# Scores of two neighbouring quads in one burst of 64 small matmuls, in a kernel with two attentions

## The chip, the cores and the metric

The kernel runs on one core of a Trainium2 chip. Its time is that of one launch on the device, in microseconds (us), and the median of several launches counts. A core has a matrix engine (PE, with the loading of weights shown as PEld), a vector engine (DVE), a scalar engine (ACT), GpSimd (POOL), and the sync engine (SP), which here issues nearly all transfers to sixteen DMA engines. Each works through its own list of instructions in order, and they wait for each other by semaphores.

## The reference

Two attention blocks, A and B, on 16 batches of 32 tokens with 1024 features, 32 query heads of 128 and caches of 1024 keys. In A eight query heads share one of 4 key heads; in B each of the 32 heads has its own. Their outputs stand side by side.

```python
q = (x @ wq).reshape(B, Sq, H, Dh).transpose(0, 2, 1, 3)
scores = einsum("bhqd,bhkd->bhqk", q, k_cache) * Dh ** -0.5
p = softmax(scores, axis=-1)
o = einsum("bhqk,bhkd->bhqd", p, v_cache)
return o.transpose(0, 2, 1, 3).reshape(B, Sq, H * Dh) @ wo
```

B's caches are the bulk of the bytes: 128 MB of keys and as many of values (in MiB), against 16 and 16 for A and 8 for each of the four weights.

## The kernel before, in words

The unit of work is a quad: four pairs of batch and head, 4 x 32 = 128 query rows. Each attention has 128 quads, and step t of the main loop (near line 1090) takes quad t of B (`quadB_all`) and about one of A (`quadA_all`). A quad of B is two neighbouring batches times two heads; `hp` says which two of a group's four heads, so that quads t and t + 1 (t even) share their batches and differ in `hp`.

The stages of a quad are: scores into PSUM (`st_scores`: L836 for A, L856 for B), negated row maximum on DVE (L866), exp on ACT with the row sum (L879), transposes of P on PE (L891), copy of them to SBUF (L540, on ACT or DVE), P.V on PE (`st_pv`: L913 for A, L921 for B), scaling by one over the sum (L937 on ACT, L938 on DVE), transpose of the output (L943) and its copy. After four quads of B or eight of A the output projection (L712) is accumulated in SBUF (L723, L726).

*B's keys.* Two K buffers belong to a quad (512 KB each; eight in all, `NKB_SLOTS`), loaded by L781. DVE transposes each buffer in place in 32 x 32 blocks (L815). The score matmuls are small, 32 rows by 32 columns of weights with 512 columns streamed: query rows from `QR`, one `tile_position` of PE's 4 x 4 grid of 32 x 32 tiles each. A quad is 32 of them, as four program entries of eight: entry `fp` goes over two batches, two heads and two halves of the keys. Row group `2 * hh + g2` and column group `2 * t_ + hh` make eight of the sixteen tiles, the same eight for every quad:

```python
for t_ in range(2):
    for hh in range(2):
        cg = 2 * t_ + hh
        for g2 in range(2):
            rg = 2 * hh + g2
```

*B's values.* Three V buffers of 1 MB (`NVB_SLOTS`), two transfers each, L794. Quad t + 2's V is loaded once quad t - 1's P.V has read its buffer. K of quad t + 4 is loaded once quad t's scores have read theirs.

*PSUM.* Two buffers of two banks hold scores (`ps_s`) and are used in turn by all quads of A and B; four banks (`ps_g`) serve all the rest.

*The order.* Nothing runs in the order written. Every operation is recorded with its reads and writes, and `Prog.list_schedule` sorts them by a table of expected durations (`DUR`), priorities from the longest path of users, and an estimate of the transfers; a copy may go to ACT or DVE (`"any"`). At each choice it takes, of the operations that can start within `LOOK` of the earliest, the one with the highest priority, with a penalty for changing PE's tile shape (`PE_MODE`, `MODE_SWITCH`). The result fixes each engine's list, and `finalize` puts in the waits. SP's list is in order too: a transfer whose buffer isn't free holds up those behind it.

*Q projection.* It is cut into units (`qprojA_head`, L624; `qprojB`, L643), each of eight matmuls of 512 columns; the lists `QB0`, `QA0`, `QB1`, `QA_T`, `QB_T` give the steps at which the units of the next heads are recorded.

Of the kernel before, what the change touches and what calls it, by code (L numbers as in the profile page):

```python
# [18 lines left out]
NKB_SLOTS = 8  # L19
LAZY_PER_STEP = 100  # L20
LAZY_DELAY = 4
WQ_DELAY = 1
A_STEPS_FRAC = 0.97
SP_STRICT = False
# [3 lines left out]
PRIO_BONUS = {}  # L28
PE_MODE = {"scoresB": 2, "Qshuf": 2, "Qshuf2": 2, "PVB": 1}
MODE_SWITCH = 0.05  # L30
LOOK = 0.35
STEP_US = 3
STEP_NEAR = 0
# [1 line left out]
TAIL_GAIN = 1.0  # L35
TAIL_BASE = 12.0
QB0 = [0, 3, 6, 9]
QA0 = [13 + (i * 9) // 8 for i in range(8)]
QB1 = [24 + (i * 9) // 8 for i in range(8)]
QA_T = [3 + (i * 12) // 8 for i in range(8)]  # L40
QB_T = [18 + (i * 12) // 8 for i in range(8)]
ACT_FIRST = 0.3


DUR = {
    "scoresB": (0.216, 0.20), "scoresA": (0.216, 0.20), "PT_trA": (0.49, 0.22), "PT_trB": (0.49, 0.22), "PVA": (0.45, 0.22), "PVB": (0.112, 0.22),
    "OT_tr": (0.056, 0.22), "KTA_tr": (0.45, 0.22), "Qshuf": (0.15, 0.20), "Qshuf2": (0.15, 0.20), "qprojA": (0.432, 0.20), "qprojB": (0.432, 0.20),
    "oprojA": (0.432, 0.20), "oprojB": (0.432, 0.20), "xT_tr": (0.45, 0.22),
    "exp": (1.10, 0.12), "PT_ev@act": (0.466, 0.13), "norm@act": (0.25, 0.13), "OT_ev@act": (0.11, 0.13), "KTA_ev@act": (0.466, 0.13),
# [66 lines left out]
class Prog:  # L116
# [118 lines left out]
    def list_schedule(self, lat=0.05, look=LOOK):  # L235
# [87 lines left out]
        def sw(i):  # L323
            if ops[i].eng != "pe":
                return 0.0
            return MODE_SWITCH if PE_MODE.get(ops[i].name, 0) != pe_mode[0] else 0.0

        def occ(i, eng):
            return dict(ops[i].alts)[eng] if ops[i].alts else ops[i].dur
        while True:  # L330
            best = None
            bkey = None
            for eng, lst in ready.items():
                if not lst:
                    continue
                fe = free.get(eng, 0.0)
                if eng == "sp":
                    fe = max(fe, dma_free[0] - SP_AHEAD)
                if eng == "dve":
                    fa = free.get("act", 0.0)  # L340
                    lst = [i for i in lst if not ops[i].alts or max(ready_t[i], fa) > max(ready_t[i], fe) + ACT_FIRST]
                    if not lst:
                        continue
                at = {}
                for i in lst:
                    s_ = slot_time(i) if acq[i] else 0.0
                    if s_ is not None:
                        at[i] = max(ready_t[i], fe, s_) + sw(i)
                if not at:
                    continue  # L350
                emin = min(at.values())
                cand = [i for i in at if at[i] <= emin + look]
                ci = max(cand, key=lambda i: (bl[i] - 8.0 * sw(i), -i))
                st = at[ci]
                end = st + occ(ci, eng)[0] if ops[ci].alts else st
                key = (st, end, -bl[ci])
                if bkey is None or key < bkey:
                    bkey = key
                    best = (ci, eng)
            if best is None:  # L360
                break
            best, beng = best
            op = ops[best]
            for x in engines(op):
                ready[x].remove(best)
            chosen[best] = beng
            st = max(ready_t[best], free.get(beng, 0.0), slot_time(best) if acq[best] else 0.0) + sw(best)
            acquire(best, st)
            if beng == "sp":
                st = max(st, dma_free[0] - SP_AHEAD)  # L370
            if beng == "pe":
                pe_mode[0] = PE_MODE.get(op.name, 0)
            op.t0 = st
            if op.dma_key is not None:
                free[beng] = st + DMA_ISSUE
                xs = max(st + DMA_FIRST, dma_free[0])
                dma_free[0] = xs + dma_time(op)
                op.t1 = dma_free[0] + DMA_LAST
            else:
                oc, tl = occ(best, beng)  # L380
                free[beng] = st + oc
                op.t1 = st + oc + tl
            release(best, op.t1 + lat)
            order.append(best)
            for u in users[best]:
                uo = ops[u]
                same_pe = (op.dma_key is None and beng == uo.eng and uo.eng == "pe" and uo.name != "Qshuf2")
                r = free[beng] if same_pe else op.t1 + lat
                if uo.dma_key is not None:
                    r += DMA_MARGIN.get(uo.name, DMA_MARGIN_DEFAULT)  # L390
                if r > ready_t[u]:
                    ready_t[u] = r
                ndeps[u] -= 1
                if ndeps[u] == 0:
                    make_ready(u)
# [54 lines left out]
def build(nc, pa, pb, out):  # L450
# [34 lines left out]
    with stack:  # L485
# [212 lines left out]
        def oproj(pi, blk, G):  # L698
# [3 lines left out]
            OT = OTA_sb if pi == 0 else OTB_sb  # L702
            wo_ = woA_sb if pi == 0 else woB_sb
            wo_res = "woA" if pi == 0 else "woB"
            lazy_flush(("wo", pi, blk))
            for oh in range(NOH):
                v = Virt("bank", "pj")
                for h0_ in range(0, nh, 2):
                    def e_op(e, oh=oh, h0_=h0_, v=v):
                        last = None  # L710
                        for hh in range(h0_, h0_ + 2):
                            last = e.matmul(bank(v)[:, 0:OUTW], OT[:, gp, hh, :], wo_[:, hh, oh * OUTW:(oh + 1) * OUTW],  # L712
                                            start=(hh == 0), stop=(hh == nh - 1))
                        return last
                    pr.add("pe", e_op, reads=[("OT", pi, gp, h0_), ("OT", pi, gp, h0_ + 1), (wo_res, h0_), (wo_res, h0_ + 1)], writes=[v],
# [106 lines left out]
                self.idx = idx  # L822
                self.res = [("bank", 2 * idx), ("bank", 2 * idx + 1)]

        def st_scores(q):
            q.vS = SBuf(s_rr[0] % 2)
            s_rr[0] += 1
            q.vP, q.vPT, q.vst, q.vO = Virt("P"), Virt("PT"), Virt("stat"), Virt("O")
            q.vbt, q.vbo = Virt("bank"), Virt("bank")
            vS = q.vS  # L830
            if q.pi == 0:
                sl = q.kvslot
                qt = QT_sb[:, q.s % 2]

                for u in range(2):
# [1 line left out]
                                                         KTA_sb[:, sl, u * 512:(u + 1) * 512], start=True, stop=True),  # L837
                           reads=[("QT", q.s % 2, q.hh0 + a) for a in range(4)] + [("KTA", sl)], writes=vS.res, name="scoresA", dur=0.225,
                           tag="A%d" % q.t, rtag=dict([(("QT", q.s % 2, q.hh0 + a), q.s) for a in range(4)] + [(("KTA", sl), q.kid)]))
            else:  # L840
                gp = (q.m * NG + q.G) % 2

                def e_s(e, fp):
                    last = None
                    if True:
                        f, pd = fp // 2, fp % 2
                        o0 = f * 64 + pd
                        for t_ in range(2):
                            a = 2 * q.bp + t_
                            for hh in range(2):  # L850
                                cg = 2 * t_ + hh
                                for g2 in range(2):
                                    rg = 2 * hh + g2
                                    lhsT = QR[32 * rg:32 * rg + 32, gp, a, q.hp, o0:o0 + 63:2]
                                    rhs = KB_sb[32 * rg:32 * rg + 32, q.ks[t_], :].rearrange("p (s x) -> p s x", s=16)[:, :, o0:o0 + 63:2]
                                    last = e.matmul(ps_s[32 * cg:32 * cg + 32, vS.idx, g2, :].rearrange("p (s j) -> p s j", s=16), lhsT, rhs,  # L856
                                                    start=(fp == 0), stop=(fp == 3), tile_position=(32 * rg, 32 * cg))
                    return last
                for fp_ in range(4):
                    pr.add("pe", lambda e, fp_=fp_: e_s(e, fp_), reads=[("QR", gp, 2 * q.bp), ("QR", gp, 2 * q.bp + 1), ("KB", q.ks[0]), ("KB", q.ks[1])],  # L860
                           writes=vS.res, name="scoresB", dur=0.275, tag="B%d" % q.t,
                           rtag={("QR", gp, 2 * q.bp): (q.m, q.G), ("QR", gp, 2 * q.bp + 1): (q.m, q.G), ("KB", q.ks[0]): ("T", q.kid), ("KB", q.ks[1]): ("T", q.kid)})

        def st_max(q):
            vS, vst = q.vS, q.vst
# [37 lines left out]
        def st_pv(q):  # L903
# [12 lines left out]
            else:  # L916
                def e_pv(e, c0):
                    last = None
                    for c in range(c0, c0 + 2):
                        for a in range(4):  # L920
                            last = e.matmul(bank(vb)[32 * a:32 * a + 32, 0:Dh], ptc_of(vPT, c, 32 * a, 32 * a + 32), VB_sb[:, kvs, a // 2, a % 2, c, :],  # L921
                                            start=(c == 0), stop=(c == NCH - 1), tile_position=(0, 32 * a))
                    return last
                for c0 in range(0, NCH, 2):
# [43 lines left out]

        def quadB_all(q):
            t = q.t  # L970
            for t_ in range(2):
                st_ktrB(q, t_)
            if t >= 1 and t - 1 + NVB < NIT:
                st_dmaV(quadsB[t - 1 + NVB])
            if t in (0, 1) and t + 2 < NIT:
                for t_ in range(2):
                    st_dmaK(quadsB[t + 2], t_)
            st_scores(q)
            if t + NKB // 2 < NIT:
                for t_ in range(2):  # L980
                    st_dmaK(quadsB[t + NKB // 2], t_)
            st_max(q)
            st_exp(q)
            st_ptr(q)
# [6 lines left out]
        def quadA_all(q):  # L991
            t = q.t
            if q.kv_new:
# [5 lines left out]
                        st_dmaK(n3)  # L999
                if n1 is not None and t >= 1:  # L1000
                    st_dmaV(n1)
            st_scores(q)
            st_max(q)
            st_exp(q)
            st_ptr(q)
# [150 lines left out]
```

## Time and profile before

| | |
|---|---|
| three runs, median | 889.17 us (888.12 to 889.93) |
| the profiled execution, its own time | 889.07 us |
| its span, first to last instruction | 887.3 us |
| granted TensorE clock, mean | 0.996 |
| HBM read, written | 337.64 MB, 2.10 MB |
| issue to landing, median, of a K or V transfer of B | 12.5, 12.2 us |
| shortest | 7.3, 7.0 us |

The profile page gives the busy time of each engine, the span in 40 slices (a digit is the busy share in tenths, and below them the GB/s that the DMA engines moved), the DMA queues, the chain of work that ended last, and groups of instructions by line: busy time, mean duration of one in ns, and the idle time just before them with what ended it. Busy time of matmuls is merged where they overlap. An answer by stretches has in each row the stretch, its length, busy time and count for PE, PEld, DVE, ACT and POOL, the granted clock, the DMA share and GB/s. A timeline row has start, length, engine, line, operation, tile and how many instructions are merged in it.

### The profile page before, as it was taken

The page shows a single profiled execution, that of the slowest core. Times are in us where ns is not written, and L with a number is a line of the kernel's source. Part 1 is how long each engine was busy: PE and PEld are TensorE (multiplying, and loading weights), DVE is VectorE, ACT ScalarE, POOL GpSimd, SP SyncE. Part 2 cuts the span into 40 slices and gives each one's busy share as a digit, 9 for nine tenths or more (in the row PEclk, how much of TensorE's full clock was granted, in tenths as well). Part 3 has the DMA queues.
Part 4 walks back from the last instruction along what each step waited for, and adds up shares of the span by engine and source line. Part 5 has one row for each costly group of instructions (what it writes and reads, how often), then busy time and mean ns, then how long its engine had stood idle before and what let it go on. Part 6 is the DMA issues. An engine that isn't in the chain of part 4 may idle for free.

```text
span 887.3 us, 29315 instructions
## 1 busy us (share of the span) xinstructions
PE 817.8 (92%) x12864; PEld 468.8 (53%) x12864; DVE 737.1 (83%) x1027; ACT 609.4 (69%) x1350; POOL 5.1 (1%) x15
## 2 busy tenths in 40 slices
PE   6999999999999999999999999999999887988986
PEld 3355555556555555555555455554555544554643
DVE  0498987879987888888898888898989888898985
ACT  3487886776767576775776677676767766676763
POOL 0000000000000000000000000000000000000000
PEclk9999999999999999999999999999999999999999
DMA  8999999999999999999999999999999999999995
GB/s 316 397 395 391 394 393 396 390 392 395 394 381 387 396 394 387 385 392 395 395 392 394 389 394 396 369 395 393 395 396 364 392 395 395 395 395 389 397 395 207
DMA packets 144830, 341.65 MB, mean 385 GB/s; under 512 B 12032, under 2 KB 12032, under 8 KB 144704
## 3 DMA queue, kind: packets, MB, share of 16 engines
q1 hardware_dynamic: 144144, 337.95, 100.6%
q8 instruction: 101, 1.65, 0.8%
q0 software_dynamic: 560, 1.84, 0.5%
q14 instruction: 25, 0.20, 0.1%
HBM read 337.64 MB, written 2.10 MB: 383 GB/s over the span
## 4 chain that ended last, share of the span: by engine, by line
PE 56%; DMA 19%; DVE 10%; ACT 8%; SPq 4%; issue 1%; ACTq 0%; DVEq 0%
DMA KB_sb<-in_B_k_cache_dram 16%; PE ps_s L856 12%; PE ps_g L891 9%; PE ps_g L712 8%; ACT P_sb L879 5%; PE ps_g L921 5%; PE ps_g L624 5%; DVE stat L866 5%; DVE KB_sb L815 4%; PE ps_g L643 4%; PE ps_g L913 4%; PE ps_s L836 4%; PE ps_g L807 2%; SPq L794 2%; PE ps_g L943 1%; ACT PT_sb L540 1%
## 5 line engine op out<-in xcount | busy, mean ns | idle before, releaser
L866 DVE TENSOR_REDUCE stat<-ps_s 128x1 f32<-128x1024 f32 x256 | 305.6, 1208 | 53.9 <-PE ps_s L856 44.5
L815 DVE STREAM_TRANSPOSE KB_sb<-KB_sb 128x1024 f32<-128x1024 f32 x256 | 309.4, 1229 | 36.6 <-DMA KB_sb<-in_B_k_cache_dram 34.4
L879 ACT ACTIVATE P_sb<-ps_s,stat 128x1024 bf16<-128x1024 f32 x256 | 286.4, 1120 | 58.8 <-DVE stat L866 57.1
L891 PE MATMUL ps_g<-id,P_sb 128*128 128x128 f32 x1024 | 172.9, 296 | 10.8 <-ACT OTA_sb L540 3.8
L856 PE MATMUL ps_s<-KB_sb,QR 32*32 32x512 bf16 x4096 | 159.1, 396 | 20.9 <-ACT P_sb L879 15.3
L891 PEld LDWEIGHTS ps_g<-id,P_sb 128*128 128x128 f32 x1024 | 148.8, 207 | 49.4 <-issue 8.3
L540 ACT COPY PT_sb<-ps_g 128x512 f32<-128x512 f32 x238 | 138.2, 593 | 46.9 <-PE ps_g L891 45.8
L937 ACT ACTIVATE O_sb<-ps_g,stat 128x128 bf16<-128x128 f32 x189 | 68.9, 371 | 64.0 <-PE ps_g L921 36.8
L921 PE MATMUL ps_g<-VB_sb,PT_sb 128*32 128x128 bf16 x4096 | 90.7, 222 | 4.6 <-ACT PT_sb L540 2.2
L836 PE MATMUL ps_s<-KTA_sb,QT_sb 128*128 128x512 bf16 x256 | 87.1, 383 | 4.6 <-ACT P_sb L879 4.4
L856 PEld LDWEIGHTS ps_s<-KB_sb,QR 32*32 32x32 bf16 x4096 | 47.4, 89 | 82.5 <-ACT P_sb L879 24.1
L921 PEld LDWEIGHTS ps_g<-VB_sb,PT_sb 128*32 128x32 bf16 x4096 | 59.8, 97 | 52.9 <-issue 36.8
L913 PE MATMUL ps_g<-VA_sb,PT_sb 128*128 128x128 bf16 x1024 | 77.6, 220 | 3.6 <-DMA VA_sb<-in_A_v_cache_dram 1.3
L913 PEld LDWEIGHTS ps_g<-VA_sb,PT_sb 128*128 128x128 bf16 x1024 | 60.9, 98 | 32.0 <-issue 13.4
L643 PE MATMUL ps_g<-wq_sb,xT_sb 128*128 128x512 bf16 x256 | 73.2, 390 | 3.5 <-DMA wq_sb<-in_B_wq_dram 3.5
L712 PE MATMUL ps_g<-woB_sb,OTB_sb 128*128 128x512 bf16 x256 | 68.1, 380 | 2.7 <-ACT PT_sb L540 1.3
L712 PE MATMUL ps_g<-woA_sb,OTA_sb 128*128 128x512 bf16 x256 | 63.0, 380 | 1.2 <-DVE OTA_sb L540 0.6
L943 PE MATMUL ps_g<-ident,O_sb 128*128 128x128 bf16 x256 | 52.3, 223 | 4.9 <-ACT O_sb L937 4.2
L624 PE MATMUL ps_g<-xT_sb,wq_sb 128*128 128x512 bf16 x192 | 55.5, 380 | 0.8 <-DMA wq_sb<-in_A_wq_dram 0.5
L879 ACT ACTIVATION_READ_ACCUMULATOR P_sb<-ps_s,stat 128x1 f32 x256 | 51.9, 203 | 0.0
L723 DVE TENSOR_TENSOR acc<-acc,ps_g 128x512 f32<-128x512 f32 x64 | 41.0, 676 | 9.9 <-PE ps_g L712 9.6
L540 ACT COPY OTA_sb<-ps_g 128x64 f32<-128x64 f32 x114 | 24.6, 217 | 35.5 <-PE ps_g L943 34.9
(43 smaller groups left out, 515.0 us busy)
## 6 DMA issues: line engine op xcount, KB each, us to landing
VB_sb<-in_B_v_cache_dram SPq DMA_DIRECT2D x256, 512.0 KB, 12.2
KB_sb<-in_B_k_cache_dram SPq DMA_DIRECT2D x256, 512.0 KB, 12.5
KA_sb<-in_A_k_cache_dram SPq DMA_DIRECT2D x64, 256.0 KB, 12.3
VA_sb<-in_A_v_cache_dram SPq DMA_DIRECT2D x64, 256.0 KB, 12.3
wq_sb<-in_B_wq_dram SPq DMA_DIRECT2D x16, 512.0 KB, 10.5
woB_sb<-in_B_wo_dram SPq DMA_DIRECT2D x32, 256.0 KB, 11.2
woA_sb<-in_A_wo_dram SPq DMA_DIRECT2D x32, 256.0 KB, 10.6
wq_sb<-in_A_wq_dram SPq DMA_DIRECT2D x12, 512.0 KB, 11.4
```

Source lines behind the costliest of these rows:

```text
L540: return e.copy(dst, src) if hasattr(e, "activation") else e.tensor_copy(dst, src)
L624: last = e.matmul(bank(v)[:, 0:tn], w_[:, j, hh * Dh:(hh + 1) * Dh], xT_sb[:, 0, j, t0:t0 + tn], start=(j == 0), stop=(j == DJ - 1))
L643: last = e.matmul(bank(v)[:, 0:CW], xT_sb[:, 1, j, G * P:(G + 1) * P], wq_sb[:, j, mh * CW:(mh + 1) * CW], start=(j == 0), stop=(j == DJ - 1))
L712: last = e.matmul(bank(v)[:, 0:OUTW], OT[:, gp, hh, :], wo_[:, hh, oh * OUTW:(oh + 1) * OUTW], start=(hh == 0), stop=(hh == nh - 1))
L815: pr.add("dve", lambda e: e.transpose(KB_sb[:, sl, :].bitcast(F32), KB_sb[:, sl, :].bitcast(F32)), writes=[("KB", sl)], name="KBt_tr", rta ...
L836: pr.add("pe", lambda e, u=u: e.matmul(ps_s[:, vS.idx, u, :], qt[:, q.b, q.hh0:q.hh0 + 4, :].rearrange("p a q -> p (a q)"), KTA_sb[:, sl, ...
L856: last = e.matmul(ps_s[32 * cg:32 * cg + 32, vS.idx, g2, :].rearrange("p (s j) -> p s j", s=16), lhsT, rhs, start=(fp == 0), stop=(fp == 3 ...
L866: pr.add("dve", lambda e: e.tensor_reduce(stat[:, vst.idx, 0:1], ps_s[:, vS.idx, :, :], AXIS.XY, ALU.max, negate=True), writes=vS.res + [v ...
L879: return e.activation(dst, src, ACTF.Exp, bias=stat[:, vst.idx, 0:1], scale=1.0, accum_out=stat[:, vst.idx, 1:2])
L891: last = e.transpose(bank(vb)[:, m * P:(m + 1) * P], p32[:, m:Sk // 2:NPK], id32[:])
L913: last = e.matmul(bank(vb)[:, 0:Dh], ptc_of(vPT, c, 0, P), VA_sb[:, kvs, c, :], start=(c == 0), stop=(c == NCH - 1))
L921: last = e.matmul(bank(vb)[32 * a:32 * a + 32, 0:Dh], ptc_of(vPT, c, 32 * a, 32 * a + 32), VB_sb[:, kvs, a // 2, a % 2, c, :], start=(c == ...
```

## The change

Line numbers above are those of the kernel before.

1. B's scores of quads t and t + 1 (t even, below `PAIR_END` = 120) are recorded together, in four entries of sixteen matmuls. For `hp` = 1 the two heads change places in the column groups, so that the second quad uses the eight tiles that the first leaves. The last eight quads are done one by one. The four K transposes stand ahead of both, the four K loads of quads t + 4 and t + 5 behind both. The burst writes both score buffers.
2. With the heads of every second quad swapped, P.V reads V with `(a % 2) ^ q.hp`, and B's output projection takes the rows of `wo` by `head_of`.
3. The scheduler counts the instructions of PE's operations (`PE_INSTR`) and adds a wait where they run past a block of 252 sooner than 6.2 us behind the block before.
4. The expected duration of an entry of B's scores goes from 0.216 to 0.33 us (for sixteen matmuls instead of eight).
5. The units of the Q projection are recorded over more steps.

```diff
-QA0 = [13 + (i * 9) // 8 for i in range(8)]
-QB1 = [24 + (i * 9) // 8 for i in range(8)]
-QA_T = [3 + (i * 12) // 8 for i in range(8)]
-QB_T = [18 + (i * 12) // 8 for i in range(8)]
+QA0 = [13 + (i * 12) // 8 for i in range(8)]
+QB1 = [27 + (i * 13) // 8 for i in range(8)]
+QA_T = [10 + (i * 11) // 8 for i in range(8)]
+QB_T = [23 + (i * 15) // 8 for i in range(8)]
...
+        def fetch_wait(i, st, commit=False):
+            if ops[i].eng != "pe" or not FETCH_US:
+                return 0.0
+            n_ = PE_INSTR[ops[i].name]
+            p0 = pe_pos[0]
+            ex = 0.0
+            b = p0 // FETCH_BLOCK + 1
+            while b * FETCH_BLOCK <= p0 + n_ - 1:
+                tb = st + ex + ops[i].dur[0] * (b * FETCH_BLOCK - p0) / n_
+                a = pe_have.get(b, 0.0)
+                if a > tb:
+                    ex += a - tb
+                    tb = a
+                if commit:
+                    pe_have[b + 1] = tb + FETCH_US
+                b += 1
...
                         at[i] = max(ready_t[i], fe, s_) + sw(i)
+                        at[i] += fetch_wait(i, at[i])
...
+                oc += fetch_wait(best, st, True)
...
+        def st_scoresB(qs):
...
+                for q in qs:
+                    for t_ in range(2):
+                        a = 2 * q.bp + t_
+                        for hh in range(2):
+                            cg = 2 * t_ + (hh ^ q.hp)
+                            for g2 in range(2):
+                                rg = 2 * hh + g2
...
+            for fp_ in range(4):
+                pr.add("pe", lambda e, fp_=fp_: e_s(e, fp_), reads=qr + [r_ for r_, _ in kt], writes=[r_ for q in qs for r_ in q.vS.res],
...
+            both = [q, quadsB[t + 1]] if t < PAIR_END and t % 2 == 0 else [q] if t >= PAIR_END else []
+            if both:
+                for p_ in both:
+                    for t_ in range(2):
+                        st_ktrB(p_, t_)
...
+                st_scoresB(both)
+                for p_ in both:
+                    if p_.t + NKB // 2 < NIT:
+                        for t_ in range(2):
+                            st_dmaK(quadsB[p_.t + NKB // 2], t_)
```

## Prediction

> **What bounds the kernel now.** I read the page's busy shares and slices first, then busy time by stretches of 20 and of 2 us, then the waits of the DMA queue, then the timeline where the DMA slackens.
>
> ```profile
> PE 817.8 (92%) x12864; PEld 468.8 (53%) x12864; DVE 737.1 (83%) x1027; ACT 609.4 (69%) x1350; POOL 5.1 (1%) x15
> ...
> GB/s 316 397 395 391 394 393 396 390 392 395 394 381 387 396 394 387 385 392 395 395 392 394 389 394 396 369 395 393 395 396 364 392 395 395 395 395 389 397 395 207
> ...
> q1 hardware_dynamic: 144144, 337.95, 100.6%
> ...
> PE 56%; DMA 19%; DVE 10%; ACT 8%; SPq 4%; issue 1%; ACTq 0%; DVEq 0%
> ```
>
> PE is the busiest engine and holds most of the chain that ended last, so it looks like the bound. The third line says otherwise: the loads fill the sixteen DMA engines for the whole span, at 390 to 396 GB/s in nearly every slice. No transfer is removed by the change, so the time is the bytes over that rate plus the moments when the queue has nothing to do. 341.65 MB at 395.5 GB/s (the usual stretch) is 863.9 us; the span is 887.3. In stretches of 2 us the missing 23 us lie so: 4.3 us in the first 10 us, 9.0 us between 10 and 868, 11.3 us behind 868 (by rate against 395.5, rounded by the last stretch).
>
> Of the middle part, only six stretches have a DMA share under 0.95: at 252 (333 GB/s), 352 (307), 560 (291) and 666 to 672 (229, 312, 347). Against 393 GB/s they lose 2 x (0.153 + 0.219 + 0.260 + 0.417 + 0.206 + 0.117) = 2.7 us. The rest is slightly lower rate at a full share, which no engine can mend. The largest of them, first by stretch, then DMA issue, then PE:
>
> ```profile
> 664.00:666.00 2.00, 2.00 (x23) 0.75 (x24) 0.80 (x1) 0.88 (x2) 0.00 (x0) 1.00 1.00 391
> 666.00:668.00 2.00, 2.00 (x37) 0.67 (x35) 1.97 (x3) 0.69 (x2) 0.00 (x0) 1.00 0.63 229
> ```
> ```profile
> 659.62 2.58 SPq L781 DMA_DIRECT2D KB_sb<-in_B_k_cache_dram  x2
> 666.79 1.91 SPq L794 DMA_DIRECT2D VB_sb<-in_B_v_cache_dram  x2
> ```
> ```profile
> 663.58 0.41 PE L921 MATMUL ps_g<-VB_sb,PT_sb 128*32 128x128 bf16 x16
> 663.92 0.66 PE L856 MATMUL ps_s<-KB_sb,QR 32*32 32x512 bf16 x16
> 664.51 1.90 PE L712 MATMUL ps_g<-woA_sb,OTA_sb 128*128 128x512 bf16 x8
> 666.34 0.41 PE L921 MATMUL ps_g<-VB_sb,PT_sb 128*32 128x128 bf16 x16
> ```
>
> The next V transfer needs a buffer that the P.V products (L921) empty. SP stands from 662.2 to 666.8 for it while PE, without a gap, does half of them, then scores, then eight output projection matmuls, then the other half. So a late PE is what starves the DMA. The same queue waits on L921 for 5.4 us at the dip at 252 and 5.5 us at 352, and on scores (L856) for 3.3 us at 560.
>
> **The change, part by part.**
>
> *Scores in one burst.* Nothing is removed: 4096 score matmuls before and after. Their arrangement changes.
>
> ```profile
> L856 PE MATMUL ps_s<-KB_sb,QR 32*32 32x512 bf16 x4096 | 159.1, 396 | 20.9 <-ACT P_sb L879 15.3
> ...
> L856 PEld LDWEIGHTS ps_s<-KB_sb,QR 32*32 32x32 bf16 x4096 | 47.4, 89 | 82.5 <-ACT P_sb L879 24.1
> ```
>
> In the timeline an unbroken quad is 32 matmuls in 1.12 to 1.14 us: four rounds, each on eight tiles at once. Two quads take 2.24 us. On sixteen tiles the 64 matmuls take between 1.12 us (all at once) and 2.24 us (no gain). No row shows sixteen. At the start of a burst 16 weight loads stand within 0.17 us, so 64 need 0.7 us and do not bind; this puts it near the lower end and I take 1.3 us. 60 pairs x 0.94 = 56 us of PE's 818 freed (bounds 0 and 67). In the instruction order 58 of the pairs stand as one unbroken run of 64; before, the scores lay in 198 runs.
>
> This does not shorten the path by 56 us, because the DMA is the path. It is worth what a late PE costs the DMA: at most the 2.7 us of dips, and part of the end. Between 868 and 878 the rate is 328, 320, 326, 196, 149 GB/s: 3.3 us lost against 393. The last two V transfers are issued at 868.88, once the fourth-last quad's P.V is done. PE has no long gap from there to 882, so arriving with less backlog helps; but the last eight quads are not paired, so the work of the end is the same. I take 2.0 us of the dips and 1.5 us of the end.
>
> A rule of the Trainium skill speaks against the burst: "TensorE: Matmul & The Clock Gate", Part 3, The mechanism, lets a weight load overlap running matmuls only when its row group differs. The burst puts four tiles on each row group in place of two. By that rule the present quad, with 8 matmuls in turn per row group at 0.217 us, would already take 1.74 us; the trace has 1.12.
>
> *K buffers held longer.* The first quad's two K buffers now wait until the second quad's are transposed, and four come free together where two did. No row prices it; it is 0 while the queue is full. Counted in the order of instructions of both programs: the bytes queued between the last transfer that a DMA issue's release needs, and that issue. For K the mean falls from 9.00 to 7.68 MB, for B's V from 6.43 to 5.94 MB; issues with less than 4 MB rise from 7 (all in the first 50 us, or the store at the end) to 19, the smallest of mid-run being 3.15 MB. 3.15 MB at 393 GB/s is 8.0 us. The chain it must cover, from rows: transpose 1.23, burst 1.3, max 1.21, exp 1.12 + 0.20, P transposes 0.75, copy 0.59, P.V 0.63 = 7.0 us. It fits by 1 us, if nothing stands in front. On SP the four K issues stand behind one wait for the burst, and V and A's transfers behind them, in order. I take 0 and keep 14 us (below) as the other end.
>
> *Both score buffers at once.* The burst waits for two exps where a quad waited for one; meanwhile max and exp have nothing from PSUM for the burst's 1.3 us. DVE (83%) and ACT (69%) have room: 60 x 1.3 = 78 us against 150 us of DVE's idle time. I take 0. Behind the waiting burst on PE stand P transposes and P.V of other quads, and for those the V transfers.
>
> *Instruction fetch in the scheduler.* It changes order only. The page's instruction queue has 101 packets for 1.65 MB, which is 64 bytes for each of PE's 25,728 instructions, so about 255 a packet. In the stretch from 60 to 80 us PE took 730 instructions (7 us a packet) at 19.65 us busy: no stall at that density. A burst is 128 instructions in 1.3 us, and two P.V add 128; denser than the trace shows. A stall costs PE between 0 and, at 1 us a pair, the whole gain of 56 us; taken as 0, since a pair's period of 13.8 us holds 402 instructions, 1.6 packets.
>
> *Q units spread, new head order.* The 256 projection units move to other steps; number and duration (0.43 us a pair of matmuls) stay. The swapped heads in P.V and output projection change addresses, not work. 0. The weight transfers of the Q projection move with them past K and V on SP; 24 of the 745 issues are theirs behind the start, and the bytes are the same.
>
> Sum: 889.07 (profiled execution: span 887.3 and 1.8 around it; the median of the three runs is 889.17) - 2.0 - 1.5 = **885.5 us**. If all 2.7 and 3.3 came back and 2 us of the lower rates, 881.
>
> **Rivals.** What a measurement of this kernel can tell from no change is about 0.2%, 1.8 us.
>
> *A, forecast: PE catches up, the dips go.* For it: the dips each end on PE. Against: only 6 us are to be had. 885.5 us, own range 881 to 887.3. Chance 0.45.
>
> *B: nothing reaches the end.* The burst frees PE, but fetch stalls or a burst waiting for two exps give it back (1 us a pair is enough), or new dips replace old ones. For it: the DMA wall, 97% of the span. 889 us, 887.3 to 890.9. Chance 0.20.
>
> *C, the other side: K buffers held by pairs starve the DMA.* Twelve more issues than before have under 4 MB of cover. One max or one exp (1.2 us) ahead in the queue uses the 1 us to spare; twelve times 1.2 is 14 us. With half of them, 889 + 7 = 896 us. It decides from the third lost place on (3 x 1.2 = 3.6, the whole gain). For it: fewer bytes of cover nearly everywhere, and DVE at 83% with transposes and maxes now bunched. Against: the median load lands 12.2 us after issue with the shortest at 7.0, so some 5 us of queue can be used up before engines idle. Chance 0.32.
>
> *D: tiles of one row group go in turn.* A matmul of 512 columns follows the last by (1.90 - 0.38) / 7 = 0.217 us in the eight L712 above. A pair is 16 matmuls a row group x 0.217 = 3.5 us, 1.2 us more than now; 60 pairs are 74 us, PE's busy time passes the span (892 us), and with today's 69 us of gaps the time is about 960 us. The present 1.12 us a quad speaks against it. Chance 0.03. The skill's rule named above is this one.
>
> So faster 0.45, same 0.20, slower 0.35. The range that leaves out no more than 2 in 10 is **881 to 897**.
>
> **What will show it.** Burst: 64 score matmuls in 1.2 to 1.4 us; 2.2 falsifies the first step. PE busy near 760 us. Dips: no 2 us stretch between 10 and 868 with a share under 0.9; SP's waits on P.V shorter. Cover: median landing of K and V below 12 us, say 10 to 11, as the queue runs emptier. If C holds, there will be a row of dips of 1 to 3 us, each ended by a V or K transfer that waited for a score burst or P.V just behind one. A PE that sits idle with "issue" inside bursts would show the fetch. A head or an end other than today's by more than 2 us would break the sum.

## The result, and the profile after

The changed kernel takes 898.74 us (median of 5 runs, 895.05 to 901.17) against 889.17: ratio 1.0103, 95% interval 1.0087 to 1.0119. It is 1% slower, clear of noise, where 885.5 was forecast, and 1.7 us above the range. From the page after (busy time, the rate by slices, the chain that ended last, the landing of B's V):

```profile
PE 757.8 (85%) x12731; PEld 474.5 (53%) x12864; DVE 744.2 (83%) x1058; ACT 601.3 (67%) x1319; POOL 5.0 (1%) x15
...
GB/s 322 397 395 392 393 394 330 395 376 371 396 396 390 395 391 394 393 391 393 395 383 388 394 391 390 350 392 394 393 395 385 395 392 395 396 375 389 385 396 161
...
DMA 33%; PE 29%; DVE 21%; ACT 8%; SPq 5%; issue 3%; POOLq 0%; POOL 0%; DVEq 0%
...
VB_sb<-in_B_v_cache_dram SPq DMA_DIRECT2D x256, 512.0 KB, 9.7
```

By this page PE is 60 us less busy. Part of that is missing records: the page counts 12731 of the 12864 matmuls (the number behind the x), the page before all of them. The run `s9_halftr` below has the same order of instructions, and all of its matmuls are in the trace:

```profile
PE 771.2 (86%) x12864; PEld 475.2 (53%) x12864; DVE 620.6 (70%) x1058; ACT 598.2 (67%) x1319; POOL 5.0 (1%) x15
```

So the change relieves PE of about 47 us. The time went to the DMA: slices of 330, 376, 371, 350 GB/s. In stretches of 2 us, against 393 GB/s, the part between 10 us and the last 20 us loses 11.9 us where it lost 3.6, and the end 12.1 where it lost 10.6; the start gives 0.5 back. That adds up to 9.3 us, and the spans differ by 9.5. Stretches with a share under 0.95 are 16 in place of 6. On the chain PE fell from 56% to 29%, DVE rose from 10% to 21%. V lands 9.7 us after issue, not 12.2: the queue runs emptier.

The burst itself is what it should be. Rows of the timeline after (start, length, engine, line, operation, tile, count) at the dip at 570, SP first, then PE, and the rate there by stretches:

```profile
566.51 0.33 SPq L821 DMA_DIRECT2D VA_sb<-in_A_v_cache_dram  x1
571.86 0.89 SPq L827 DMA_DIRECT2D VB_sb<-in_B_v_cache_dram  x2
```
```profile
568.09 0.52 PE L961 MATMUL ps_g<-VB_sb,PT_sb 128*32 128x128 bf16 x24
568.54 1.90 PE L745 MATMUL ps_g<-woA_sb,OTA_sb 128*128 128x512 bf16 x8
570.37 1.21 PE L895 MATMUL ps_s<-KB_sb,QR 32*32 32x512 bf16 x64
571.51 0.29 PE L961 MATMUL ps_g<-VB_sb,PT_sb 128*32 128x128 bf16 x8
```
```profile
568.00:570.00 2.00, 2.00 (x33) 1.05 (x32) 0.94 (x1) 1.24 (x3) 0.00 (x0) 1.00 0.93 367
570.00:572.00 2.00, 2.00 (x77) 1.11 (x75) 1.95 (x3) 0.31 (x3) 0.00 (x0) 1.00 0.51 205
572.00:574.00 2.00, 1.84 (x25) 1.47 (x24) 2.00 (x3) 1.30 (x4) 0.00 (x0) 1.00 0.64 218
```

64 score matmuls take 1.21 us. SP stands from 566.8 to 571.9 for the V transfer, because the quad whose V buffer is wanted has its last eight P.V matmuls (L961) behind eight of the output projection and the burst. It is the picture at 666 us before, with the burst in it; the DMA falls to half of its rate at 570.

Why PE comes to P.V late is seen on DVE and in the waits. DVE's rows after the burst that ended at 186.1 us:

```profile
186.15 1.23 DVE L906 TENSOR_REDUCE stat<-ps_s 128x1 f32<-128x1024 f32 x1 [1.12 <-PE ps_s L895]
187.29 2.36 DVE L848 STREAM_TRANSPOSE KB_sb<-KB_sb 128x1024 f32<-128x1024 f32 x2
189.58 1.19 DVE L906 TENSOR_REDUCE stat<-ps_s 128x1 f32<-128x1024 f32 x1
190.69 2.35 DVE L848 STREAM_TRANSPOSE KB_sb<-KB_sb 128x1024 f32<-128x1024 f32 x2
192.96 1.19 DVE L906 TENSOR_REDUCE stat<-ps_s 128x1 f32<-128x1024 f32 x1
```

DVE stood idle for 1.12 us until the burst ended. Then two score buffers wait at once. By the instruction order the three maxima are those of the pair's first quad, of a quad of A and of the pair's second quad: that one is through at 194.15, 8.0 us behind the burst, since four K transposes of later quads come first. (From one to four such transposes stand between the two maxima of 26 of the 60 pairs, all four in six of them.) With DVE's list laid against the traces, a quad's maximum before ends 1.7 us behind its scores in the mean of all 128; the second maximum of a pair ends 4.4 us behind the burst. Its score buffer is full all that time, so A's scores wait for exp. PE's waits for a score buffer (engine, tile, line, releaser: us in total, times, longest) before, and after:

```profile
PE ps_s L856 <- ACT P_sb L879: 15.3, 19, 1.7
...
PE ps_s L836 <- ACT P_sb L879: 4.4, 7, 1.9
```
```profile
PE ps_s L872 <- ACT P_sb L919: 32.7, 45, 2.1
...
PE ps_s L895 <- ACT P_sb L919: 8.9, 21, 1.2
```

Ahead of A's scores (L836, then L872) that is 4.4 us against 32.7; ahead of B's (L856, then L895) it falls from 15.3 to 8.9. So it is not the burst itself that stands longer, but A's scores and all that comes behind them on PE: 41.6 us in all, 19.7 before. SP's waits for P.V before a V transfer grow too, before and after:

```profile
SPq L794 <- PE ps_g L921: 67.5, 33, 5.5
```
```profile
SPq L827 <- PE ps_g L961: 214.8, 87, 5.8
```

### The profile page after: what moved, and what is told of

The parts are those of the page before. It is cut to its first block, busy times and chain, and to the rows that moved or that the text cites. A ratio compares the mean times of both kernels' runs of the same rounds, so it can differ in the third digit from the quotient of the medians.

```text
span 896.8 us, 29178 instructions
## 1 busy us (share of the span) xinstructions
PE 757.8 (85%) x12731; PEld 474.5 (53%) x12864; DVE 744.2 (83%) x1058; ACT 601.3 (67%) x1319; POOL 5.0 (1%) x15
## 4 chain that ended last, share of the span: by engine, by line
DMA 33%; PE 29%; DVE 21%; ACT 8%; SPq 5%; issue 3%; POOLq 0%; POOL 0%; DVEq 0%
DMA KB_sb<-in_B_k_cache_dram 26%; DVE KB_sb L848 10%; DVE stat L906 9%; PE ps_g L931 6%; ACT P_sb L919 6%; PE ps_g L745 6%; PE ps_s L895 4%; PE ps_g L961 3%; DMA woB_sb<-in_B_wo_dram 3%; PE ps_g L953 2%; PE ps_s L872 2%; SPq L814 2%; SPq L827 2%; PE ps_g L654 2%; PE ps_g L673 2%
## 5 line engine op out<-in xcount | busy, mean ns | idle before, releaser
L931 PE MATMUL ps_g<-id,P_sb 128*128 128x128 f32 x1024 | 178.2, 301 | 14.8 <-ACT OTA_sb L570 5.2
L570 ACT COPY PT_sb<-ps_g 128x512 f32<-128x512 f32 x222 | 128.6, 591 | 53.3 <-PE ps_g L931 51.6
L872 PE MATMUL ps_s<-KTA_sb,QT_sb 128*128 128x512 bf16 x223 | 74.5, 390 | 41.6 <-ACT P_sb L919 32.7
L977 ACT ACTIVATE O_sb<-ps_g,stat 128x128 bf16<-128x128 f32 x184 | 66.6, 371 | 52.5 <-PE ps_g L961 24.6
L961 PE MATMUL ps_g<-VB_sb,PT_sb 128*32 128x128 bf16 x4096 | 89.2, 222 | 10.7 <-issue 5.2
L895 PE MATMUL ps_s<-KB_sb,QR 32*32 32x512 bf16 x4096 | 83.7, 394 | 10.2 <-ACT P_sb L919 8.9
L961 PEld LDWEIGHTS ps_g<-VB_sb,PT_sb 128*32 128x32 bf16 x4096 | 60.2, 97 | 46.6 <-issue 30.9
L953 PE MATMUL ps_g<-VA_sb,PT_sb 128*128 128x128 bf16 x1024 | 80.5, 223 | 3.9 <-ACT PT_sb L570 1.6
L673 PE MATMUL ps_g<-wq_sb,xT_sb 128*128 128x512 bf16 x223 | 64.3, 393 | 8.3 <-DMA wq_sb<-in_B_wq_dram 3.6
L895 PEld LDWEIGHTS ps_s<-KB_sb,QR 32*32 32x32 bf16 x4096 | 46.8, 89 | 38.8 <-ACT P_sb L919 20.3
L654 PE MATMUL ps_g<-xT_sb,wq_sb 128*128 128x512 bf16 x161 | 47.7, 387 | 8.6 <-DVE acc L756 3.0
L872 PEld LDWEIGHTS ps_s<-KTA_sb,QT_sb 128*128 128x128 bf16 x256 | 20.0, 99 | 64.9 <-ACT P_sb L919 59.5
## 6 DMA issues: line engine op xcount, KB each, us to landing
KB_sb<-in_B_k_cache_dram SPq DMA_DIRECT2D x256, 512.0 KB, 11.2
woB_sb<-in_B_wo_dram SPq DMA_DIRECT2D x32, 256.0 KB, 10.4
```

Source lines behind the costliest of these rows:

```text
L570: return e.copy(dst, src) if hasattr(e, "activation") else e.tensor_copy(dst, src)
L673: last = e.matmul(bank(v)[:, 0:CW], xT_sb[:, 1, j, G * P:(G + 1) * P], wq_sb[:, j, mh * CW:(mh + 1) * CW], start=(j == 0), stop=(j == DJ - 1))
L872: pr.add("pe", lambda e, u=u: e.matmul(ps_s[:, vS.idx, u, :], qt[:, q.b, q.hh0:q.hh0 + 4, :].rearrange("p a q -> p (a q)"), KTA_sb[:, sl, ...
L895: last = e.matmul(ps_s[32 * cg:32 * cg + 32, q.vS.idx, g2, :].rearrange("p (s j) -> p s j", s=16), lhsT, rhs, start=(fp == 0), stop=(fp == ...
L931: last = e.transpose(bank(vb)[:, m * P:(m + 1) * P], p32[:, m:Sk // 2:NPK], id32[:])
L953: last = e.matmul(bank(vb)[:, 0:Dh], ptc_of(vPT, c, 0, P), VA_sb[:, kvs, c, :], start=(c == 0), stop=(c == NCH - 1))
```

## The experiments

Each was run with the kernel before on the same chip; ratios are to it. My theory after the result: a pair makes the chain from K's landing to the release of V too long for the buffers, by (a) waiting for both score buffers and filling both, and (b) holding the first quad's K. The rivals: the scheduler's counting or the Q units cost it; only K's buffers do; it is the place of P.V in PE's list.

**Which part of the change** (`s1_single`, `s4_nofetch`, `s5_oldq`).

```diff
-PAIR_END = 120          # s1_single; with 0.216 us and 16 instructions expected
+PAIR_END = 0
-FETCH_US = 6.2          # s4_nofetch
+FETCH_US = 0
-QA0 = [13 + (i * 12) // 8 for i in range(8)]     # s5_oldq; QB1, QA_T, QB_T likewise
+QA0 = [13 + (i * 9) // 8 for i in range(8)]
```

> Changed kernel with every quad scored alone again (PAIR_END 0, an entry of eight matmuls, 0.216 us and 16 instructions expected); the swapped heads, the counting of fetches and the spread of the Q units stay. If pairing costs the time (by the burst or by the K buffers), this is within 0.3% of the kernel before, 889 us, and the dips of the DMA between 10 us and the end fall from 10 us to about 3. If the scheduler's counting or the Q units cost it, it stays at 896 to 900.

888.83 us, ratio 0.9999 (0.9990 to 1.0009); the middle loses 4.1 us. The pairing is the cost; swapped heads, counting and Q units cost nothing without it.

> Changed kernel, the scheduler's counting of instruction fetches switched off (FETCH_US 0). If the order that the counting makes costs time, 890 to 895. If it shields PE from real stalls, more than 900, with idle PE put down to nothing but issue inside runs of small matmuls. If it matters in neither way, 897 to 900.

898.29 us, 1.0099 (1.0074 to 1.0124). The counting matters in neither way: the time is that of the changed kernel. It does shorten stalls: PE's idle time ahead of P.V put down to "issue" is 13.4 us (longest 2.1) without it and 5.2 (1.6) with it.

> Changed kernel with the Q units at the steps of the kernel before. If their new places cost the time at 140 to 200 us, where three of the longest dips lie, 893 to 896. If the pairing alone is at fault, 897 to 901 with dips elsewhere.

914.53 us, 1.0271 (1.0244 to 1.0298): worse by 16 us, against both expectations. The new places of the Q units are needed by the pairs; they win back more than the pairing still costs. The dips lie elsewhere, as at 414 (99 GB/s) and 892 (37 GB/s). What in the old places hurts was not tried apart.

**Which part of the pairing** (`s2_hold`, `s6_couple`, `s3_nine`). In both of the first two, a quad has its own four entries of eight matmuls:

```diff
+            for q in qs:
+                own = [(("KB", q.ks[t_]), ("T", q.kid)) for t_ in range(2)]
...
+                    pr.add("pe", ..., reads=qr + [r_ for r_, _ in kt], writes=q.vS.res, ...)    # s2_hold
+                    pr.add("pe", ..., reads=qr + [r_ for r_, _ in own], writes=[r_ for p_ in qs for r_ in p_.vS.res], ...)    # s6_couple
-NKB_SLOTS = 8           # s3_nine
+NKB_SLOTS = 9
```

> Pairs are recorded as in the changed kernel, and each quad's scores read all four K buffers of the pair, so K is held as long as in the changed kernel; but each quad has four entries of eight matmuls of its own and waits for its own score buffer alone. Theory 'K buffers held': as slow as the changed kernel, 896 to 900. Theory 'burst waits for both score buffers': 888 to 892.

901.55 us, 1.0139 (1.0120 to 1.0157).

> The other half: each quad's scores read its own two K buffers alone, so the first quad's K is free early, but both quads' scores wait for both score buffers, as the burst does (in entries of eight matmuls, 2.24 us a pair on PE if the two quads' matmuls don't run at once, 1.2 if they do). Theory 'burst waits for both score buffers': 896 to 902. Theory 'K buffers held': 888 to 892.

909.30 us, 1.0234 (1.0205 to 1.0263). Either half of the pairing alone is slower than the whole, so neither theory may stand alone. The two are not sums of the whole: each has an order of its own, and gives PE little of the relief (828 and 798 us busy, against about 771). The first has no entry on sixteen tiles and is slower still, so these as such are not the cost.

> Changed kernel with nine K buffers in place of eight, the ninth of 512 KB. Theory 'K buffers held': half of the 9.6 us comes back, 891 to 895, and fewer dips. Theory 'burst waits for both score buffers' (V buffers come free late behind it): no change, 897 to 900.

896.23 us, 1.0076 (1.0054 to 1.0097). By the ratios 0.27% of the time comes back, 2.4 us, a quarter. The two intervals overlap, and this run has an order of its own, so a part of K's holding is likely and not shown.

**The length of the chain, in an unchanged order** (`s9_halftr`, `s12_halfscore`, `s13_both`, with controls). These leave the instruction order as it is and do half of the work of one stage.

```diff
-e.transpose(KB_sb[:, sl, :].bitcast(F32), KB_sb[:, sl, :].bitcast(F32))       # s9_halftr, s9b_before_halftr
+e.transpose(KB_sb[:, sl, 0:8 * Dh].bitcast(F32), KB_sb[:, sl, 0:8 * Dh].bitcast(F32))
-e.tensor_reduce(stat[:, vst.idx, 0:1], ps_s[:, vS.idx, :, :], ...)            # s12_halfscore, s12b_before_halfscore
+e.tensor_reduce(stat[:, vst.idx, 0:1], ps_s[:, vS.idx, 0:1, :], ...)          # exp likewise over 512 keys
```

> Changed kernel, same order of instructions on every engine, but each in-place transpose of K does half of the buffer (0.62 us in place of 1.23; the other half stays as loaded, so the scores are not the reference's). Theory 'DVE's bunched transposes and maxes make the chain from K's landing to P.V too long for the buffers': the dips go, 884 to 890. Theory 'PE or the burst itself': 896 to 900.

893.41 us, 1.0046 (1.0030 to 1.0062). About half of the loss comes back, though PE's waits for a score buffer are nearly as long (38.8 us against 41.6).

> Control of the half transposes: the kernel before in its own order, each in-place transpose of K over half of the buffer (the other half stays as loaded, so the scores are not the reference's). If the 5.3 us that they gave the changed kernel belong to its pairing, this gains 2 us at most, 887 to 889. If any relief of DVE helps every order alike, 883 to 885.

888.74 us, 0.9993 (0.9983 to 1.0004).

> Changed kernel in its own order, maximum and exp over half of the keys (the other half of P is zeros, so the result is not the reference's), which lets go of a score buffer about 1.2 us earlier per quad. Theory 'score buffers coupled by the burst': the waits of A's scores for exp fall from 92 us to under 40 and the time to 884 to 889. Theory 'K buffers held': 894 to 897, as K's chain keeps its transposes.

893.23 us, 1.0045 (1.0030 to 1.0061). PE's waits for a score buffer, 41.6 us in the changed kernel, fell to 14.9, below the 19.7 of the kernel before: 2.9 ahead of B's scores and 12.0 ahead of A's, in the row below. (The 92 us of the expectation add the waits of the weight loads to those of the matmuls, which overlap in time; on that count A's fell to 37.8.)

```profile
PE ps_s L875 <- ACT P_sb L922: 12.0, 16, 1.6
```

The time did not follow as far: 893, not 884 to 889.

> Control of the half maximum and exp: the kernel before in its own order, with the same part left out. If the score buffers bind only in pairs, 885 to 889.

888.61 us, 0.9993 (0.9983 to 1.0004). Half a transpose takes 0.70 us in place of 1.23, half a maximum 0.67, half an exp 0.69. So 0.5 us less per K transpose is worth more than half of the loss to the paired order and nothing to the single one, and the same holds for maximum and exp.

> Changed kernel in its own order with K transposes, maximum and exp all over half of the data (what they leave out is said at the two runs before). If DVE's and ACT's part of the chain is the whole loss, the two halves of about 5.4 us add up: 887 to 889. If the rest is where the release of V stands in PE's list (behind a burst), the same places keep their dips: 891 to 893.

891.51 us, 1.0039 (1.0024 to 1.0055). They don't add up: each removes much the same half, and 0.4% stays with both. The dips at 198, 566 and 790 are still there.

**The place of P.V, and more V buffers** (`s14_pvprio6` with control, `s15_pvwhole`, `s10_v4`).

```diff
-PRIO_BONUS = {}                                  # s14_pvprio6, s14b_before_pvprio
+PRIO_BONUS = {"PVB": 6.0}
-                for c0 in range(0, NCH, 2):      # s15_pvwhole: one entry of 32 matmuls
-SLOTS = {"bank": 4, "P": 3, "PT": 3, "stat": 6, "O": 2}
+SLOTS = {"bank": 4, "P": 2, "PT": 2, "stat": 6, "O": 2}    # s10_v4, with NVB_SLOTS = 4
```

> Changed kernel, the scheduler gives the P.V of B 6 us more priority, so that fewer quads' P.V have a burst between their parts (5 of 128 in place of 10 in the instruction order). Theory 'V comes free behind a burst': 890 to 894. Theory 'only the chain on DVE and ACT': 897 to 900.

978.77 us, 1.1015 (1.0978 to 1.1051).

> Control: the kernel before with the same priority for P.V. 887 to 890 if its order is not limited there; under 887 it would be better than both kernels.

968.66 us, 1.0916 (1.0885 to 1.0947). This priority spoils either order, so the pair of runs says nothing of the theory.

> Changed kernel with each quad's 32 P.V matmuls of B as one entry (in place of four), so that no burst stands between them. Theory 'V comes free behind a burst': 890 to 895. Theory 'only the chain on DVE and ACT': 897 to 902.

902.60 us, 1.0163 (1.0145 to 1.0180). No burst can stand inside a quad's P.V here, and it is no faster: no sign that the split is at fault. Counted in the instruction order, scores stand between the parts of a quad's P.V in 10 of 128 quads of the changed kernel and in 38 of the kernel before, so the split is not what pairing brought.

> Changed kernel with four V buffers in place of three, and two buffers in place of three for P and for its transpose to make room. The queue's longest waits are V transfers behind P.V (215 us in all). If more V in flight covers the late P.V, 889 to 893; if the K buffers bind as well, 895 to 898; fewer P buffers may cost what it brings, 899 and more.

909.52 us, 1.0221 (1.0200 to 1.0243). Two numbers of buffers differ here, and the order with them; what a fourth V buffer is worth by itself stays open, as there was no room for it.

**Is PE's relief worth anything, and what is left?** (`s7_before_nine`, `s16_before_halfburst`, `s17_both_nine`).

```diff
-rhs = KB_sb[...].rearrange("p (s x) -> p s x", s=16)[:, :, o0:o0 + 63:2]
+rhs = KB_sb[...].rearrange("p (s x) -> p s x", s=16)[:, 0:8, o0:o0 + 63:2]   # s16_before_halfburst
```

> The kernel before with nine K buffers. Its dips end on V transfers that wait for P.V, so little: 887 to 889. If K buffers bind there too, 884 to 886, and a better kernel than both.

889.01 us, 0.9997 (0.9985 to 1.0008).

> The kernel before in its own order, each score matmul of B over 256 columns in place of 512 (the other half of the score buffer stays as it was, so the scores are not the reference's). PE is freed of about as much as the bursts free it, and nothing is paired. The prediction's term 'PE catches up': 885 to 887. Theory 'the DMA wall leaves nothing to win': 888 to 890.

888.23 us, 0.9996 (0.9987 to 1.0006). From its page, busy time and chain, and then the busy time of `s9b_before_halftr`, which has the same order and full score matmuls:

```profile
PE 759.8 (86%) x12696; PEld 474.1 (53%) x12864; DVE 738.5 (83%) x1029; ACT 608.4 (69%) x1350; POOL 5.0 (1%) x15
...
DMA 38%; PE 30%; DVE 14%; ACT 9%; SPq 7%; issue 2%; ACTq 0%; DVEq 0%
```
```profile
PE 798.2 (90%) x12696; PEld 470.1 (53%) x12864; DVE 612.9 (69%) x1027; ACT 608.9 (69%) x1350; POOL 5.0 (1%) x15
```

The same 168 matmul records are missing in both, so PE is relieved of about 38 us, less than the 47 of the bursts. Its share of the chain falls from 56% to 30%, and the time stays. The middle loses 4.2 us where it lost 3.6, the end 9.9 where it lost 10.6.

> Changed kernel with the halves of transposes, maximum and exp as at the run before, and nine K buffers. If what those halves left (2.5 us) is K held by the pair: 888 to 890. If not: 891 to 893.

891.83 us, 1.0042 (1.0026 to 1.0059): a ninth K buffer wins back none of the 0.4% left. No version beat both kernels.

## Why the prediction was wrong, step by step

- *The DMA is the bound*: right. Relief of PE, of DVE or of ACT, and a ninth K buffer, each left the kernel before at 0.9993 to 0.9997.
- *The burst, 1.3 us taken, 56 us of PE freed*: right for the burst, 1.21 us; PE is freed of about 47 us. That the page has "near 760", as the prediction asked, is owed to its missing records. Of the rule of the Trainium skill ("TensorE: Matmul & The Clock Gate", Part 3, The mechanism) that a weight load overlaps matmuls of other row groups only: sixteen matmuls in turn on each row group at 0.217 us would be 3.5 us a pair; the trace has 1.21 and goes against it.
- *"I take 2.0 us of the dips and 1.5 us of the end"*: **this step failed.** A relief of 38 us without pairing moved the time by -0.04% (interval -0.13% to +0.06%), 0.3 us, where 3.5 were taken for 56. The dips at 254 and 666 stay with it.
- *"Both score buffers at once ... I take 0"*: **failed.** DVE's idle time in total (150 us) was set against the 78 us of waiting, but the idle time is not where the wait falls. Nor does the wait fall on the burst, which stands for less time than the single scores did: PE waits 28 us more ahead of A's scores, and SP 147 us more for P.V. Maximum and exp at half their length win back about 5 us of the 9.6.
- *"K buffers held longer ... I take 0"*: **failed as well.** The chain that I added up for its cover (7.0 us against 8.0) has a maximum of 1.21 us right behind the burst; a pair's second maximum ends 4.4 us behind it in the mean, 8 in the rows above. Transposes of half the length win back about 5 us. They and the maxima are parts of one chain and remove much the same half, so which of the two terms is the larger stays open; a ninth K buffer brings some 2.4 us, at the edge of noise.
- *Rival C* named the side, a DMA starved by buffers that pairs hold, and its signs (transfers waiting for P.V behind a burst; V and K transfers behind a burst or P.V, landing 10 to 11 us; measured 9.7 for V, 11.2 for K), but its count of places does not carry: of the mid-run issues with under 4 MB of cover, those at 150 and 201 us in the trace are at dips, those at 71, 113, 265 and 849 are not, one at 158 comes behind a dip, and the V transfer at the dip at 570 has 5.0 MB. Its price of 7 us was 2.6 short: the middle lost 8.3 us more and the end 1.5. It came nearest, with a chance of 0.32 against 0.45 for the forecast.
- *Instruction fetch in the scheduler and swapped heads at 0*: right. *Q units at 0*: right for single quads, but without their spread the pairs lose 2.7%.
- *The end "the same"*: nearly. The last V transfer, issued at 869.3 us and landed at 878.6 before, is issued at 878.0 and lands at 886.3; that is 7.8 of the 9.5 us between the spans. Behind it 10.4 us follow, 8.7 before.

Open: the 0.4% that is left with transposes, maxima and exps halved (`s13_both`). The score buffers are not all of it: PE waits 22.7 us for them there, near the 19.7 of before, while SP still waits 167.8 us for P.V before V transfers (67.5 before). What halving doesn't change is DVE's list. A pair's second maximum still stands behind K transposes, and these now wait for K itself to land; their rows after and in `s13_both`, with the idle time ahead of them last:

```profile
L848 DVE STREAM_TRANSPOSE KB_sb<-KB_sb 128x1024 f32<-128x1024 f32 x256 | 308.7, 1228 | 46.5 <-DMA KB_sb<-in_B_k_cache_dram 43.9
```
```profile
L851 DVE STREAM_TRANSPOSE KB_sb<-KB_sb 128x512 f32<-128x512 f32 x256 | 180.3, 708 | 221.1 <-DMA KB_sb<-in_B_k_cache_dram 220.7
```

With the list laid against the traces, 2.8 us of this wait lie between the two maxima of a pair after, and 34.6 in `s13_both`; the second maximum ends 4.4 us behind the burst after and still 3.7 there. That is a candidate for the rest, not shown: no run moves the second maximum ahead of the transposes. And most runs have a schedule of their own; that alone can move the time by much (the old places of the Q units: +16 us), so only those in an unchanged order are read as prices.

## What to carry to other kernels

Before pricing a faster burst, ask which stretch of the bound it shortens: here transfers ran almost without a gap, and taking 38 us of work off an engine at 92%, which held most of the chain, moved the time by 0.04%. And a batch that needs two buffers at once turns a pipeline into steps: price it by how long a buffer stays full and by what waits behind it in the in-order lists, not by the idle time in total. Test it by shortening the suspected stage in an unchanged order, with the same cut in the old kernel as a control.

## What was not expected of the hardware

The granted TensorE clock fell to 0.50 in eight spells of 3 to 7 us, two before. Stretches around one (the third number from the end is the clock):

```profile
840.00:842.00 2.00, 1.21 (x41) 0.69 (x42) 2.00 (x3) 1.83 (x3) 0.00 (x0) 1.00 1.05 400
842.00:844.00 2.00, 1.39 (x7) 0.98 (x7) 2.00 (x5) 1.72 (x5) 0.00 (x0) 0.71 1.02 380
844.00:846.00 2.00, 2.00 (x16) 1.85 (x14) 1.74 (x3) 1.69 (x3) 0.00 (x0) 0.50 1.03 373
```

The spell lasts from 842.8 to 846.3 us. In the 3.4 us ahead of it PE was busy for 1.95, with gaps of 0.8 and 0.5 us. The Trainium skill ("TensorE: Matmul & The Clock Gate", Part 1) has the half clock after an idle window of about 3.4 us; here no idle gap was that long (the longest of PE in this execution, 3.05 us at 346.5, has no spell behind it). It was not the loss: the run with PE relieved and nothing paired has eleven such spells and the time of before, and of the long dips after only that at 794 is at one.
